# Block-causal attention with a gated FFN: q's and k's last 64 tokens in one tile and one transpose, and a planner that counts TensorE's weight loads

## The chip, the cores and the metric

The kernel runs on one core of a Trainium2 chip. The metric is the time of one execution on the device, in microseconds (us). The time before is 800.11 us, the median of three runs (797.95 to 801.85).

## What is computed

Eight batches of eight heads attend over 576 tokens with 64 dimensions per head. A token sees its own block of 64 and all earlier ones. The heads' results, side by side, are the 512-wide input of a feed-forward net: a matmul to 1024, a ReLU, a convolution over three neighbouring tokens whose sigmoid gates the ReLU's output, and a matmul back to 512.

```python
scores = scale * np.matmul(q, k.transpose(0, 1, 3, 2))
mask = block_i >= block_j                    # blocks of 64 tokens
attn = softmax(np.where(mask, scores, -1e9))
x = np.matmul(attn, v)                       # heads side by side: (8, 576, 512)
h = np.maximum(x @ w_in, 0.0)
conv_out = sum(conv_w[k] * hp[:, k:k + S, :] for k in range(3))
out = (h * sigmoid(conv_out)) @ w_out
```

## The kernel before

**Number format.** TensorE multiplies in fp32r. Where that is too coarse, a value is kept as a high part and a low part (`qh` and `ql`, `kh` and `kl`, `xh` and `xl`, `gh` and `gl`, and so on), and a product is summed from two or three matmuls.

**Visits.** Two heads together (a pair) are 128 partitions wide. The work on one pair is a visit. The first batch's four pairs are visited twice, for the tokens up to 256 (part A) and for the rest (part B), so that work can begin while the FFN's weights still arrive. The other 28 pairs have one visit each.

**A visit.** `load_nat` (L493) loads q and k of the pair with tokens on partitions, into the buffers `qn` and `kn`, of which there is one each. 576 tokens are four chunks of 128 and a fifth of 64, so the fifth chunk's tile fills only partitions 0 to 63. `chunks` (L488, the call is L491) turns each chunk by a transpose on TensorE: the tile is the stationary operand (the weights), an identity is the moving one. For the fifth chunk weights and identity are cut to 64 rows. `stage_t` (L804) does that in four PSUM banks, two for q (chunks 0 to 2, then 3 and 4) and two for k. ScalarE copies each bank out as a high part (L824), VectorE writes the low part (L827), and DMAs that SyncE issues (L837, L846, L857) put the halves in place. In part B `rest_t` (L896) does the same for chunks 2 to 4, in one bank for q and one for k. Then come scores in four steps of 128 queries (`stage_s`, L1022 and L1024, tile `s`, two banks) and one step for the last 64 queries of both heads (`last_s`, L977), with maximum (VectorE L1032), exponential (ScalarE L1035) and normalisation (GpSimd L951); transposes of the probabilities (`stage_x`, L1208, tile `w`, three banks); and the product with V (`stage_pv`, L1299, with one short product for the last chunk, L1295). That product has a first pass with 128 columns of weights (V's high and low part side by side) and a second pass, for the probabilities' low part, with 64 columns of weights.

**The FFN.** `ffn` (L1353) makes the net's matmuls (L1375 into 1024 features, L1434 back, tile `f`) for half a batch at a time. They are `paced`: spread over the attention of the next batch.

**The planner.** Every step of all these is an `Op` with an engine, a length that formulas such as `c_mm` and `c_tr` give, and what it depends on. `Plan.forward` (L163) plays the whole program through and takes on each engine the ready step that is due first; `Plan.late` turns the result into new due times, and `order` (L151) keeps the best of 25 rounds. What comes out is the order in which each engine's instructions are written; the chip then runs each engine's queue in that order. Where the plan has TensorE idle for over 0.4 us it puts in filling matmuls that compute nothing (L1565), which keep its clock up. Before the change a matmul's planned length is that of its moving operand alone:

```python
    def c_mm(n, m=P):
        return max(n * 0.000447 + 0.005, 0.086 * m / P)

    def c_tr(n):
        return max(n * 0.083 - 0.035, 0.06)
```

In `stage_pv` the second pass is one step in the plan, or two of up to two matmuls each: `halves` (L1282, L1286).

Of the kernel before, what the change touches and what calls it, by code (L numbers as in the profile page):

```python
# [10 lines left out]
F32R = mybir.dt.float32r  # L11
# [8 lines left out]
class Op:  # L20
    __slots__ = ("eng", "dur", "lat", "fn", "deps", "target", "seq", "outs", "left", "start", "end", "paced", "port", "xfer", "area", "rows64")
# [41 lines left out]
class Plan:  # L63
# [5 lines left out]
    SIGNAL = (0.055, 0.035, 0.035, 0.08, 0.1)  # L69
# [15 lines left out]
    def op(self, eng, dur, fn, target, deps=(), bufs=(), lat=0.0, paced=False, port=False, xfer=0.0, area=0.92,  # L85
           rows64=False):
        o = Op()
        o.xfer, o.area, o.rows64 = xfer, area, rows64
        o.port = port or eng == POOL
# [61 lines left out]
    def order(self, window, skip, fill, clock, rounds):  # L151
        best, least = None, 1e30
        for _ in range(rounds + 1):
            done = self.forward(window, skip, fill, clock)
# [8 lines left out]
    def forward(self, window, skip, fill, clock):  # L163
# [41 lines left out]
        rtime = [0.0] * len(self.ops)  # L205
        port = 0.0
# [4 lines left out]
        while left:  # L211
# [5 lines left out]
            for e in range(5):  # L217
# [26 lines left out]
            if e == PE and t - free[PE] > least and t > begin:  # L244
# [11 lines left out]
                if banks:  # L256
# [3 lines left out]
                    if k > 0:  # L260
# [3 lines left out]
                        x.area, x.rows64 = 0.91, False  # L264
                        use(x)
# [5 lines left out]
            if where == 0:  # L271
                heapq.heappop(ready[e][0 if o.port or o.paced else 1])
# [18 lines left out]
            for c in o.outs:  # L291
                c.left -= 1
                lat = self.DRAIN[e] + (self.SIGNAL[c.eng] if c.eng != e else 0.0) if (e != PE or c.eng != PE) else 0.0
                rtime[c.seq] = max(rtime[c.seq], o.end + o.lat + lat)
                if c.left == 0:
# [6 lines left out]
def kernel(  # L302
# [74 lines left out]
    ROUNDS = 24  # L377

# [48 lines left out]
    spans = [(f"p{i}", 128 * (i + 1), 2) for i in range(4)] + [("p4", S, 1), ("qn", 5 * P, 1), ("kn", 5 * P, 1)]  # L427
# [18 lines left out]
    def c_mm(n, m=P):  # L446
        return max(n * 0.000447 + 0.005, 0.086 * m / P)

    def c_tr(n):
        return max(n * 0.083 - 0.035, 0.06)  # L450
# [37 lines left out]
    def chunks(n, tb, cs):  # L488
        for z, c in enumerate(cs):
            m = P if c < 4 else 64  # L490
            nc.tensor.transpose(tb.ap[:, P * z:P * z + m].bitcast(F32R), n.raw[0:m, P * c:P * c + P], rident[0:m, 0:m])  # L491

    def load_nat(p, at, part=None):  # L493
        b, h0 = p // NP, 2 * (p % NP)
        c0 = 2 if part else 0
        res = []
        for src, tag in ((q, "qn"), (k, "kn")):
            n = twin(tag)

            def go(src=src, n=n):  # L500
                x = n.ap.rearrange("p (c j d) -> p c j d", c=5, j=2)
# [3 lines left out]
                nc.sync.dma_start(out=x[0:64, 4, :, :], in_=src[b, h0:h0 + 2, 4 * P:S, :].rearrange("j p d -> p j d"))  # L505

            res.append((n, pl.op(SP, 1.5, go, at, bufs=[n], xfer=c_dma(2 * (S - P * c0) * D * 4, 256))))
# [160 lines left out]
    def split(f, parts, src, hi, lo, scratch, deps, bufs, at, go):  # L668
# [52 lines left out]
        o2 = pl.op(PE, c_mm(512), less, at + 1, deps=[o1], bufs=[fb])  # L721
        if f in WPA:
            o2 = pl.op(PE, 4 * c_mm(512), all_, at + 1, deps=[o2], bufs=bufs + [fb])
        o2 = pl.op(PE, c_mm(512), rest, at + 1, deps=[o2] + [x[1] for x in o], bufs=bufs + [fb])
# [78 lines left out]

    def stage_t(nat, at):  # L804
# [5 lines left out]
        for which, (n, ld) in enumerate(nat):  # L810
            hi, lo = (qh, ql) if which == 0 else (kh, t["kl"])
            scale = SCALE if which == 0 else 1.0
            t0 = at + 2.0 * which
            es = []
            for j, cs in enumerate(((0, 1, 2), (3, 4))):
                tb = bank("tv")
                nn = (384, 192)[j]
                tok = slice(384 * j, 384 * j + nn)

                def tr(n=n, tb=tb, cs=cs):  # L820
                    chunks(n, tb, cs)

                def ev_hi(tb=tb, hi=hi, scale=scale, tok=tok, nn=nn):
                    nc.scalar.activation(out=hi.ap[:, tok], in_=tb.ap[:, 0:nn], func=AF.Copy, scale=scale)  # L824

                def ev_lo(tb=tb, hi=hi, lo=lo, scale=scale, tok=tok, nn=nn):
                    nc.vector.scalar_tensor_tensor(out=lo.ap[:, tok], in0=tb.ap[:, 0:nn], scalar=scale,  # L827
                                                   in1=hi.ap[:, tok], op0=ALU.mult, op1=ALU.subtract)

                o = pl.op(PE, c_tr(len(cs)), tr, t0 + 0.5 * j, deps=[ld], bufs=[n, tb], area=0.7)  # L830
                o = pl.op(ACT, c_act(nn) + 0.03, ev_hi, t0 + 0.5 * j + 0.3, deps=[o], bufs=[tb, hi])
                es.append(o)
                es.append(pl.op(DVE, c_dve(nn, two_in=True), ev_lo, t0 + 0.5 * j + 0.7, deps=[o], bufs=[tb, hi, lo]))
# [62 lines left out]
    def rest_t(nat, at):  # L896
# [4 lines left out]
        for which, (n, ld) in enumerate(nat):  # L901
            hi, lo = (t["qa"], t["qb"]) if which == 0 else (t["kh"], t["kl"])
            scale = SCALE if which == 0 else 1.0
            for j in range(1):
                tb = bank("tv")
                nn = S - Q1
                tok = slice(Q1, S)

                def tr(n=n, tb=tb):
                    chunks(n, tb, (2, 3, 4))  # L910

                def ev_hi(tb=tb, hi=hi, scale=scale, tok=tok, nn=nn):
                    nc.scalar.activation(out=hi.ap[:, tok], in_=tb.ap[:, 0:nn], func=AF.Copy, scale=scale)

                def ev_lo(tb=tb, hi=hi, lo=lo, scale=scale, tok=tok, nn=nn):
                    nc.vector.scalar_tensor_tensor(out=lo.ap[:, tok], in0=tb.ap[:, 0:nn], scalar=scale,
                                                   in1=hi.ap[:, tok], op0=ALU.mult, op1=ALU.subtract)

                t0 = at + 0.5 * (which + j)
                o = pl.op(PE, c_tr(3), tr, t0, deps=[ld], bufs=[n, tb], area=0.7)  # L920
                o = pl.op(ACT, c_act(nn) + 0.03, ev_hi, t0 + 0.3, deps=[o], bufs=[tb, hi])
                es.append(o)
                es.append(pl.op(DVE, c_dve(nn, two_in=True), ev_lo, t0 + 0.7, deps=[o], bufs=[tb, hi, lo]))
# [40 lines left out]
    def last_s(t, ready4, t0, pb, done, exps, part):  # L964
# [4 lines left out]
        for j in range(2):  # L969
# [12 lines left out]
            o = pl.op(PE, 3 * c_mm(HS), mm4, t0, deps=ready4, bufs=[sb, t["qz"], t["qdl"], t["kh"], t["kl"]])  # L982
# [17 lines left out]
    def stage_s(ops, hh, at, part, shared):  # L1000
# [9 lines left out]
        for z, i in enumerate(i for g in groups for i in g):  # L1010
# [27 lines left out]
            o = pl.op(PE, 2 * c_mm(nk) + (0.05 if i == 0 else 0) + (0.09 if pmask else 0), mm, t0, deps=ready[hh],  # L1038
# [14 lines left out]
    def stage_sb(ops, at):  # L1053
# [4 lines left out]
        for z, i in enumerate((2, 3)):  # L1058
# [15 lines left out]
            m = pl.op(PE, 3 * c_mm(nk) + 0.06, mm, t0, deps=ready, bufs=sb + [t[x] for x in ("qa", "qb", "kh", "kl")],  # L1074
# [527 lines left out]
```

## Time and profile before

| what | value |
|---|---|
| median of three runs | 800.11 us |
| the profiled execution | 800.5 us |
| its span, first to last instruction | 798.7 us |
| mean granted TensorE clock | 0.996 |
| busy: TensorE matmul (PE) | 784.3 us, 98% |
| busy: TensorE weight load (PEld) | 698.8 us, 87% |
| busy: VectorE, ScalarE, GpSimd | 642.2, 617.8, 427.4 us |
| matmuls, of them filling ones | 5307, 90 |

How to read it. A matmul is two instructions. One loads the weights (PEld in the profile), the other streams the moving operand (PE). Both engines' rows overlap, because loads go ahead of the matmul before. The end of a matmul is modelled, so "PE busy" hides short stops. What tells how fast TensorE really goes are the starts of the weight loads: in a full queue one load starts each time that one matmul makes way. A timeline row `217.76 0.42 PEld L491 LDWEIGHTS ... x2` says that a group of two loads of line 491 began at 217.76 us and that the last of them ended 0.42 us later. Shapes are rows\*columns of the weights, then the operand.

### The profile page before, as it was taken

Reading aid. Unit: us, or ns where it says so; the run is one execution under the profiler, and the core shown is the slowest. Engines: PE = TensorE matmul, PEld = TensorE weight load, DVE = VectorE, ACT = ScalarE, POOL = GpSimd, SP = SyncE. Lnnn points to the kernel's source line nnn. Section 1 sums busy time; section 2 is a strip of 40 time slices with the busy share of each in tenths; the row PEclk is TensorE's granted clock in tenths of the full one; section 3 lists DMA queues with packets and bytes.
Section 4 is the critical chain, followed back from the end, with each engine's and each line's share of the span. In section 5 each row is a group of like instructions: output and inputs, shape, how many; then the busy total and the mean of one; then the engine's idle time right before and its main releaser. Section 6 shows DMA issues by size and latency. Waiting matters only on the chain.

```text
span 798.7 us, 17165 instructions
## 1 busy us (share of the span) xinstructions
PE 784.3 (98%) x5307; PEld 698.8 (87%) x5307; DVE 642.2 (80%) x1889; ACT 617.8 (77%) x1769; POOL 427.4 (54%) x607
## 2 busy tenths in 40 slices
PE   7999999999999999999999999999999999999998
PEld 4678789888989889898989889898999989898996
DVE  6789988998988869797888869888888959887541
ACT  4779888877978769797887859787887858787652
POOL 3436545566664645555456644645565643646431
PEclk9899999999999999999999999999999999999999
DMA  9423465557555445445555454455554445540001
GB/s 247 130 56 101 119 148 122 139 124 171 124 125 137 103 115 129 112 114 121 137 132 118 98 130 111 119 124 136 128 125 106 111 111 123 126 107 15 14 27 39
DMA packets 164350, 91.34 MB, mean 114 GB/s; under 512 B 135564, under 2 KB 139684, under 8 KB 164260
## 3 DMA queue, kind: packets, MB, share of 16 engines
q1 hardware_dynamic: 163716, 90.12, 46.8%
q8 instruction: 43, 0.70, 0.4%
q14 instruction: 47, 0.39, 0.2%
q10 hardware_dynamic: 544, 0.13, 0.1%
HBM read 38.30 MB, written 9.44 MB: 60 GB/s over the span
## 4 chain that ended last, share of the span: by engine, by line
PE 91%; DVE 4%; ACT 2%; POOL 1%; DMA 1%; issue 1%; SPq 0%; ACTq 0%; POOLq 0%; DVEq 0%
PE f L1375 25%; PE f L1434 22%; PE w L1299 12%; PE w L1208 7%; PE s L1022 5%; PE s L1024 4%; PE w L491 4%; PE w L1434 4%; PE s L977 3%; PE s L1375 2%; PE s L1068 1%; DMA gh<-in_moe_w_in_dram 1%; PE s L1565 0%; PE w L1224 0%; POOL p0f L1164 0%
## 5 line engine op out<-in xcount | busy, mean ns | idle before, releaser
L1415 POOL TENSOR_TENSOR gl<-t,gh 128x288 fp32r<-128x288 f32 (+2 forms) x128 | 103.5, 812 | 148.6 <-ACT gh L1412 131.2
L1032 DVE TENSOR_REDUCE st<-s 128x1 f32<-128x128 f32 x224 | 107.1, 481 | 2.6
L1218 ACT ACTIVATE ptbh<-w 128x384 fp32r<-128x384 f32 (+2 forms) x192 | 94.5, 508 | 16.7 <-PE w L1208 15.5
L1434 PE MATMUL f<-woh,gh 128*128 128x512 f32 x248 | 103.8, 419 | 0.0
L1434 PE MATMUL f<-wol,gh 128*128 128x512 f32 x248 | 97.8, 394 | 0.0
L1434 PE MATMUL f<-woh,gl 128*128 128x512 f32 x248 | 97.8, 394 | 0.0
L1221 DVE TENSOR_TENSOR ptbl<-w,ptbh 128x512 fp32r<-128x512 f32 (+1 forms) x144 | 89.9, 628 | 9.1 <-ACT ptbh L1218 7.9
L1375 PE MATMUL f<-xh,wih 128*128 128x290 f32 (+2 forms) x480 | 95.5, 307 | 0.3 <-ACT p1f L1149 0.3
L1375 PE MATMUL f<-xh,wil 128*128 128x290 f32 (+2 forms) x480 | 95.3, 303 | 0.0
L1375 PE MATMUL f<-xl,wih 128*128 128x290 f32 (+2 forms) x480 | 92.4, 304 | 0.0
L951 POOL TENSOR_SCALAR p0f<-p0f,st 128x128 f32<-128x128 f32 x56 | 20.9, 373 | 121.4 <-DVE st L945 82.7
L1375 PEld LDWEIGHTS f<-xh,wil 128*128 128x128 f32 x480 | 73.7, 189 | 1.8 <-issue 0.2
L1396 DVE SCALAR_TENSOR_TENSOR t<-f,cw,t 128x287 f32<-128x287 f32 (+3 forms) x120 | 59.4, 496 | 19.5 <-ACT t L1392 17.9
L1375 PEld LDWEIGHTS f<-xh,wih 128*128 128x128 f32 x480 | 72.2, 189 | 2.3 <-ACT p1f L1149 0.8
L1375 PEld LDWEIGHTS f<-xl,wih 128*128 128x128 f32 x480 | 71.8, 189 | 0.9
L1024 PE MATMUL s<-kl,qz 128*128 128x128 f32 x224 | 72.1, 322 | 0.0
L1313 ACT ACTIVATE xt<-w 64x256 f32<-64x256 f32 x112 | 44.7, 402 | 29.4 <-PE w L1299 27.5
L1316 DVE TENSOR_TENSOR xt<-w,xt 64x256 f32<-64x256 f32 x112 | 51.4, 460 | 16.7 <-ACT xt L1313 13.4
L1392 ACT ACTIVATE t<-f,cw 128x288 f32<-128x288 f32 (+2 forms) x120 | 59.7, 499 | 2.7 <-ACT ptbh L1218 0.2
L1400 DVE SCALAR_TENSOR_TENSOR t<-f,cw,t 128x288 f32<-128x288 f32 (+3 forms) x120 | 60.4, 504 | 1.1
L1412 ACT ACTIVATE gh<-t 128x288 fp32r<-128x288 f32 (+2 forms) x128 | 56.3, 442 | 6.1 <-DVE t L1408 5.8
L1405 ACT ACTIVATE t<-t 128x288 f32<-128x288 f32 (+2 forms) x128 | 56.4, 442 | 5.9 <-DVE t L1400 5.3
(248 smaller groups left out, 2288.2 us busy)
## 6 DMA issues: line engine op xcount, KB each, us to landing
out_dram<-stage SPq DMA_DIRECT2D x36, 256.0 KB, 2.3
vn<-in_v_dram SPq DMA_DIRECT2D x64, 128.0 KB, 2.6
ka<-kh SPq DMA_DIRECT2D x56, 144.0 KB, 2.6
kb<-kh SPq DMA_DIRECT2D x56, 144.0 KB, 2.6
qnf<-in_q_dram SPq DMA_DIRECT2D x56, 128.0 KB, 2.5
knf<-in_k_dram SPq DMA_DIRECT2D x56, 128.0 KB, 2.7
qa<-qh SPq DMA_DIRECT2D x28, 144.0 KB, 2.4
qz<-qh SPq DMA_DIRECT2D x28, 144.0 KB, 2.6
```

The costliest lines, as they stand in the source:

```text
L1024: nc.tensor.matmul(sb.ap[:, 0:nk], qz.ap[:, z:z + 128], kl.ap[:, 0:nk], start=False, stop=True)
L1032: nc.vector.tensor_reduce(out=st.ap[:, i:i + 1], in_=sb.ap[:, 0:nk], op=ALU.max, axis=AX.X, negate=True)
L1218: nc.scalar.activation(out=hi(), in_=src(), func=AF.Copy)
L1221: nc.vector.tensor_tensor(out=lo(), in0=src(), in1=hi(), op=ALU.subtract)
L1299: nc.tensor.matmul(tb.ap[0:m, q0 - qa:qb - qa], vv.ap[:, chunk(c), hh, w[ps_]], pm.ap[:, 128 * c + q0:128 * c + qb] if qa == 0 else pm.ap[ ...
L1375: nc.tensor.matmul(fb.ap[:, 0:n2], wt[:, c, fs], xs[c][xi].ap[:, x0:x0 + n2], start=(n + c - c0 == 0), stop=(n + c - c0 == 3 * NCC - 1))
L1392: nc.scalar.activation(out=t.ap[:, 0:no], in_=fb.ap[:, own:own + no], func=AF.Copy, scale=cw[:, NFC + f:NFC + f + 1])
L1396: nc.vector.scalar_tensor_tensor(out=t.ap[:, i0:no], in0=fb.ap[:, own + i0 - 1:own + no - 1], scalar=cw[:, f:f + 1], in1=t.ap[:, i0:no], o ...
L1400: nc.vector.scalar_tensor_tensor(out=t.ap[:, 0:i1], in0=fb.ap[:, own + 1:own + 1 + i1], scalar=cw[:, 2 * NFC + f:2 * NFC + f + 1], in1=t.a ...
L1405: nc.scalar.activation(out=t.ap[:, 0:no], in_=t.ap[:, 0:no], func=AF.Tanh)
L1415: nc.gpsimd.tensor_tensor(out=gbuf[1].ap[:, f, carry:carry + no], in0=t.ap[:, 0:no], in1=gbuf[0].ap[:, f, carry:carry + no], op=ALU.subtract)
L1434: nc.tensor.matmul(fb.ap[:, 0:DM], gbuf[a].ap[:, f, cs], w[:, f, :], start=(f == 0 and n == 0), stop=(f == NFC - 1 and n == 2))
```

## The change

It has three parts.

1. **One tile for the two fifth chunks.** k's last 64 tokens are loaded into partitions 64 to 127 of q's fifth tile, and `kn` shrinks to four chunks. One transpose of 128 rows turns both; its output goes to two places of one bank, 64 columns each. `chunks` is gone; `naturals` does the transposes of both stages. `stage_t` now has three banks of three transposes (the middle one holds chunk 3 of q, the shared tile and chunk 3 of k, and is copied out in two pieces), `rest_t` a bank of three and one of two. k's load now writes into both buffers, so it also waits for the readers of `qn`.
2. **Planned lengths count weight loads.** Each matmul has a stream time and a load time (`mm_`, `tr_`); in the plan a matmul starts no earlier than its load's time after the one before it began, and a group's length is the sum over neighbours of the greater of stream and next load (`run`). Between ready steps `forward` now also looks at this: after a long stream, steps with a full-width load are brought forward by 1.0 us (`FAR`). `SIGNAL` of TensorE goes from 0.055 to 0.04. No other constant of the plan changes.
3. **V's second pass matmul by matmul.** In the visits after the first batch each matmul of the second pass is a step of its own.

```diff
-    SIGNAL = (0.055, 0.035, 0.035, 0.08, 0.1)
+    SIGNAL = (0.04, 0.035, 0.035, 0.08, 0.1)
...
+                if b and e == PE:
+                    near, far = pair if tail < 0.1 else (0.0, pair[1])
+                    b = min((x[2] for x in ready[e][1]),
+                            key=lambda o: (o.target - near if o.ldw < 0.06 else o.target - (0 if tail < 0.1 else far), o.seq))
...
             if e == PE:
+                o.start = t = max(t, max(begun, wtime[o.seq]) + o.ldw)
                 o.end = t + (o.dur + (switch if o.rows64 != rows else 0.0)) * speed(t)
+                begun, tail = o.end - o.tail * speed(t), o.tail
...
+    NEAR, FAR = 0.0, 1.0
...
-    spans = [(f"p{i}", 128 * (i + 1), 2) for i in range(4)] + [("p4", S, 1), ("qn", 5 * P, 1), ("kn", 5 * P, 1)]
+    spans = [(f"p{i}", 128 * (i + 1), 2) for i in range(4)] + [("p4", S, 1), ("qn", 5 * P, 1), ("kn", 4 * P, 1)]
...
+    def run(*mms):
+        total = sum(max(s, w) for (s, _), (_, w) in zip(mms, mms[1:])) + mms[-1][0]
+        return total, mms[0][1], mms[-1][0]
+
+    def mm_(n, m=P):
+        return 0.002 + n * 0.0004545, 0.001 + 0.000836 * m
+
+    def tr_(m=P, n=P):
+        return 0.002 + n * 0.0004545, 0.022 + 0.0005 * m
...
-    def chunks(n, tb, cs):
-        for z, c in enumerate(cs):
-            m = P if c < 4 else 64
-            nc.tensor.transpose(tb.ap[:, P * z:P * z + m].bitcast(F32R), n.raw[0:m, P * c:P * c + P], rident[0:m, 0:m])
...
-                nc.sync.dma_start(out=x[0:64, 4, :, :], in_=src[b, h0:h0 + 2, 4 * P:S, :].rearrange("j p d -> p j d"))
+                x = ns[0].ap[64 * z:64 * z + 64, 4 * P:5 * P].rearrange("p (j d) -> p j d", j=2)
+                nc.sync.dma_start(out=x, in_=src[b, h0:h0 + 2, 4 * P:S, :].rearrange("j p d -> p j d"))
...
+                for col, x, c in cs:
+                    o, m = tb.ap[:, col:col + P], rident
+                    if c == 4:
+                        o = tb.ap[:, col:col + 2 * x].rearrange("p (j n) -> p j n", j=2)[:, :, 0:64]
+                        x, m = nq, rident.rearrange("p (j n) -> p j n", j=2)
+                    nc.tensor.matmul(o.bitcast(F32R), x.raw[:, P * c:P * c + P], m, start=(col == 0), stop=True,
+                                     is_transpose=True, skip_group_check=True)
...
+        parts = ((((0, nq, 0), (P, nq, 1), (2 * P, nq, 2)), [lq], [nq], ((0, 0, 0, 384),)),
+                 (((0, nq, 3), (P, 192, 4), (192, nk, 3)), [lq, lk], [nq, nk], ((0, 0, 384, 192), (1, 192, 384, 192))),
+                 (((0, nk, 0), (P, nk, 1), (2 * P, nk, 2)), [lk], [nk], ((1, 0, 0, 384),)))
...
-                    halves = [h[::-1] for h in halves[::-1]]
+                    halves = [h[::-1] for h in halves[::-1]] if early else [[c] for c in cs[::-1]]
...
-                    cost = sum(c_mm(qb - max(128 * c, qa), m) for c in half) + (c_mm(64, m) if tailed else 0)
+                    cost = run(*([mm_(64, passes[k - 1][1])] if tailed else []), *[mm_(qb - max(128 * c, qa), m) for c in half])
```

The other changed lines of the diff put `run`, `mm_` and `tr_` in the place of `c_mm` and `c_tr`.

More of the change, by code (lines that the diff above doesn't have):

```diff
@@ L264, in forward @@
                         x.area, x.rows64 = 0.91, False
+                        begun, tail = x.end - each, each
                         use(x)
@@ L271, in forward @@
             if where == 0:
-                heapq.heappop(ready[e][0 if o.port or o.paced else 1])
+                h = ready[e][0 if o.port or o.paced else 1]
+                if h[0][2] is o:
+                    heapq.heappop(h)
+                else:
+                    h.remove(next(x for x in h if x[2] is o))
+                    heapq.heapify(h)
             else:
@@ L720, in split @@
             o1 = pl.op(ACT, c_act(512), fh, at + 1, deps=[x[0] for x in o], bufs=bufs)
-        o2 = pl.op(PE, c_mm(512), less, at + 1, deps=[o1], bufs=[fb])
+        o2 = pl.op(PE, run(mm_(512)), less, at + 1, deps=[o1], bufs=[fb])
         if f in WPA:
-            o2 = pl.op(PE, 4 * c_mm(512), all_, at + 1, deps=[o2], bufs=bufs + [fb])
-        o2 = pl.op(PE, c_mm(512), rest, at + 1, deps=[o2] + [x[1] for x in o], bufs=bufs + [fb])
+            o2 = pl.op(PE, 4 * mm_(512)[0], all_, at + 1, deps=[o2], bufs=bufs + [fb])
+        o2 = pl.op(PE, run(mm_(512)), rest, at + 1, deps=[o2] + [x[1] for x in o], bufs=bufs + [fb])
         if f in WPA:
@@ L809, in stage_t @@
         ready, ready4 = ([], []), []
-        for which, (n, ld) in enumerate(nat):
-            hi, lo = (qh, ql) if which == 0 else (kh, t["kl"])
-            scale = SCALE if which == 0 else 1.0
-            t0 = at + 2.0 * which
[L814 to L833, printed above, removed]
+        (nq, lq), (nk, lk) = nat
+        parts = ((((0, nq, 0), (P, nq, 1), (2 * P, nq, 2)), [lq], [nq], ((0, 0, 0, 384),)),
+                 (((0, nq, 3), (P, 192, 4), (192, nk, 3)), [lq, lk], [nq, nk], ((0, 0, 384, 192), (1, 192, 384, 192))),
+                 (((0, nk, 0), (P, nk, 1), (2 * P, nk, 2)), [lk], [nk], ((1, 0, 0, 384),)))
+        both = naturals(parts, nq, (qh, ql, kh, t["kl"]), (at, at + 0.5, at + 2.0))
+        for which in range(2):
+            t0 = at + 2.0 * which
+            es = both[which]
             if which == 0:
@@ L900, in rest_t @@
         es, ready4 = [], []
-        for which, (n, ld) in enumerate(nat):
-            hi, lo = (t["qa"], t["qb"]) if which == 0 else (t["kh"], t["kl"])
[L903 to L923, printed above, removed]
+        (nq, lq), (nk, lk) = nat
+        parts = ((((0, nq, 2), (P, nq, 3), (2 * P, 64, 4)), [lq, lk], [nq], ((0, 0, Q1, 320), (1, 320, 512, 64))),
+                 (((0, nk, 2), (P, nk, 3)), [lk], [nk], ((1, 0, Q1, 256),)))
+        both = naturals(parts, nq, (t["qa"], t["qb"], t["kh"], t["kl"]), (at, at + 0.5))
+        for which in range(2):
+            hi, lo = (t["qa"], t["qb"]) if which == 0 else (t["kh"], t["kl"])
+            t0 = at + 0.5 * which
+            es += both[which]
             if which == 0:
@@ L1570 @@
     ctx.enter_context(tc.manual_schedule(engines=None))
-    for o in pl.order(WINDOW, SKIP, (work, NBANK, 0.234, LEAST, SPARE), CLOCK, ROUNDS):
+    for o in pl.order(WINDOW, SKIP, (work, NBANK, 0.234, LEAST, SPARE), CLOCK, ROUNDS, (NEAR, FAR)):
         o.fn()
```

72 lines of the change are left out of this document (45 added, 27 removed).

## The prediction, made before the change was timed

> **What bounds the kernel now.** I read the page first, then busy time by stretches, then the groups by line and shape for TensorE's weight loads, and last the timeline of those loads. The page:
>
> ```profile
> span 798.7 us, 17165 instructions
> PE 784.3 (98%) x5307; PEld 698.8 (87%) x5307; DVE 642.2 (80%) x1889; ACT 617.8 (77%) x1769; POOL 427.4 (54%) x607
> ...
> PE 91%; DVE 4%; ACT 2%; POOL 1%; DMA 1%; issue 1%; SPq 0%; ACTq 0%; POOLq 0%; DVEq 0%
> ```
>
> TensorE bounds it: 91% of the chain that ended last is its work. The stretches (length, then busy us of PE, PEld, DVE, ACT, POOL, then the granted clock) tell where:
>
> ```profile
> 0.00:47.00 47.00, 40.42 (x208) 28.73 (x208) 33.48 (x98) 29.17 (x81) 20.82 (x37) 0.93 0.63 163
> 47.00:120.00 73.00, 70.01 (x498) 58.58 (x499) 66.19 (x184) 62.21 (x174) 38.74 (x62) 1.00 0.46 115
> ...
> 200.00:700.00 500.00, 499.88 (x3461) 454.72 (x3460) 417.50 (x1251) 401.32 (x1164) 280.60 (x390) 1.00 0.51 120
> ```
>
> From 200 to 700 us PE is never idle, at full clock, while VectorE is busy for 417.5 of 500 and ScalarE for 401. There each nanosecond that leaves TensorE's queue should leave the span. "Busy" still hides stops, since ends of matmuls are modelled; the starts of weight loads show them. Two healthy places, as start and length of each group of loads:
>
> ```profile
> 301.02 0.36 PEld L1208 LDWEIGHTS w<-rident,p2r 128*128 128x128 f32 x3
> 301.33 0.19 PEld L1022 LDWEIGHTS s<-ka,qa 128*128 128x128 f32 x1
> 301.44 0.19 PEld L1024 LDWEIGHTS s<-kl,qz 128*128 128x128 f32 x1
> 301.55 0.30 PEld L1375 LDWEIGHTS f<-xl,wih 128*128 128x128 f32 x2
> ...
> 302.30 0.45 PEld L1208 LDWEIGHTS w<-rident,p3r 128*128 128x128 f32 x4
> 302.69 0.30 PEld L1375 LDWEIGHTS f<-xh,wih 128*128 128x128 f32 x2
> ```
>
> Three transposes take 0.31 us to the next load (301.02 to 301.33), four 0.39 (302.30 to 302.69): 0.08 us for each further one, and so 0.14 to 0.15 for a run of one. Ordinary weights of 128 columns behind a short stream cost 0.11 (301.33, 301.44, 301.55). Now two places with a fifth chunk, a transpose of 64 rows (line 491):
>
> ```profile
> 195.05 0.14 PEld L491 LDWEIGHTS w<-rident,qnr 128*128 128x128 f32 x1
> 195.35 0.49 PEld L491 LDWEIGHTS w<-rident,qnr 64*128 64x128 f32 x4 [0.16 <-issue]
> 195.78 0.19 PEld L1434 LDWEIGHTS f<-woh,gh 128*128 128x128 f32 x1
> ...
> 217.76 0.42 PEld L491 LDWEIGHTS w<-rident,qnr 128*128 128x128 f32 x2
> 218.22 0.30 PEld L1375 LDWEIGHTS f<-xl,wih 128*128 128x128 f32 x2
> ```
>
> At 217.76 one whole and one 64-row transpose take 0.46 us where one whole takes 0.14: the 64-row one costs 0.32. At 195.05 one whole, one 64-row and three whole take 0.73 (to 195.78), against 0.39 for four whole: 0.34. The load path stands still in front of it (0.16 us, "issue": nothing is waited for) and the next load comes late too. That this holds for all 64 of them is in the groups by shape (busy, mean ns, idle before):
>
> ```profile
> L491 PEld LDWEIGHTS w<-rident,knr 128*128 128x128 f32 x120 | 14.5, 140 | 1.6 <-issue 0.2
> L491 PEld LDWEIGHTS w<-rident,qnr 128*128 128x128 f32 x120 | 14.1, 141 | 0.9
> L491 PEld LDWEIGHTS w<-rident,qnr 64*128 64x128 f32 x32 | 4.3, 136 | 4.6 <-issue 2.9
> L491 PEld LDWEIGHTS w<-rident,knr 64*128 64x128 f32 x32 | 4.3, 135 | 4.0 <-issue 0.5
> ```
>
> 8.6 us of idle stand before 64 loads of 64 rows (0.134 us each), 2.5 us before 240 loads of 128 rows (0.010 each).
>
> **The change part by part.** *The shared transpose.* It removes 64 transposes of 64 rows and adds 32 of 128 rows. In the order of TensorE at 194.5 to 195.8 us of the profile before, `qnr` and `knr` being q's and k's natural tiles:
>
> ```order
> L1295 MATMUL w<-ptbh,vv 128x64
> L1299 MATMUL w<-ptbl,vv 64x192
> L1299 MATMUL w<-ptbl,vv 64x320 x3
> L491 MATMUL w<-rident,qnr_95 128x128
> L491 MATMUL w<-rident,qnr_95 128x64
> L491 MATMUL w<-rident,qnr_95 128x128 x3
> L1434 MATMUL f<-woh,gh 128x512
> ```
>
> and the same visit in the changed kernel:
>
> ```order
> L832 MATMUL w<-rident,qnr_95 128x128
> L832 MATMUL w<-rident,qnr_95 128x2x64
> L832 MATMUL w<-rident,knr_97 128x128
> L1316 MATMUL w<-ptbh,vv 128x320 x3
> L1316 MATMUL w<-ptbh,vv 128x192
> L1312 MATMUL w<-ptbh,vv 128x64
> L1316 MATMUL w<-ptbl,vv 64x192
> L1316 MATMUL w<-ptbl,vv 64x320
> L832 MATMUL w<-rident,qnr_95 128x128 x3
> ```
>
> The 64-wide tail of q (and k's, further on) is gone, and the middle bank, with the 2x64 output, holds both. Removed: 64 x 0.32 = 20.5 us (19.2 to 21.8 by 0.30 and 0.34). Added: 32 x 0.08 = 2.6 us, since all rows are now 128. Net -17.9 us. At the least, if only the idle time in front goes and the 32 fewer loads, it is 8.6 + 32 x 0.08 = 11.2 us. 56 of the 64 belong to the 28 visits after the first batch, where TensorE bounds all.
>
> Here the Trainium skill bears on the row: "TensorEngine Tiling (Array Packing)", section Tiling Modes, says that a change of the tiling mode, not merely of the tile, drains TensorE. Row and rule agree that going to 64 rows and back stops the queue. The same page counts weights of 64 columns as another mode too; by that the next part would cost stops. The trace speaks against it:
>
> ```profile
> 324.43 0.38 PEld L1208 LDWEIGHTS w<-rident,p2r 128*128 128x128 f32 x3
> 324.75 0.19 PEld L1299 LDWEIGHTS w<-ptbl,vv 128*64 128x64 f32 x2
> 324.95 0.19 PEld L1434 LDWEIGHTS f<-woh,gh 128*128 128x128 f32 x1
> 325.09 0.19 PEld L1434 LDWEIGHTS f<-wol,gh 128*128 128x128 f32 x1
> ```
>
> *V's second pass.* Here two loads of 64 columns follow a transpose with no stop. They take 0.20 us together. The second interval streams 320 columns, as the next one does (324.95 to 325.09, 0.14); so the first took 0.06. Behind a transpose a narrow load costs 0.06 where a wide one costs 0.11. In the order such places rise from 13 to 40: 27 x 0.05 = -1.4 us. TensorE near 188.4 to 190.5 us, before (`p0r` to `p3r` probabilities, `vv` V):
>
> ```order
> L1295 MATMUL w<-ptbh,vv 128x64
> L1299 MATMUL w<-ptbl,vv 64x192
> L1299 MATMUL w<-ptbl,vv 64x320 x3
> L1208 MATMUL w<-rident,p0r_79 128x128
> L1208 MATMUL w<-rident,p1r_83 128x128 x2
> L1022 MATMUL s<-ka,qa 128x384
> L1024 MATMUL s<-kl,qz_127 128x384
> L1208 MATMUL w<-rident,p2r_87 128x128 x3
> L1434 MATMUL f<-woh,gh 128x512
> L1434 MATMUL f<-wol,gh 128x512
> L1434 MATMUL f<-woh,gl 128x512
> L1022 MATMUL s<-ka,qa 128x512
> ```
>
> and now:
>
> ```order
> L1312 MATMUL w<-ptbh,vv 128x64
> L1316 MATMUL w<-ptbl,vv 64x192
> L1316 MATMUL w<-ptbl,vv 64x320
> L1225 MATMUL w<-rident,p0r_79 128x128
> L1225 MATMUL w<-rident,p1r_83 128x128 x2
> L1316 MATMUL w<-ptbl,vv 64x320
> L1039 MATMUL s<-ka,qa 128x384
> L1041 MATMUL s<-kl,qz_127 128x384
> L1225 MATMUL w<-rident,p2r_87 128x128 x3
> L1316 MATMUL w<-ptbl,vv 64x320
> L1039 MATMUL s<-ka,qa 128x512
> ```
>
> The three narrow products have moved apart, each behind a run of transposes.
>
> *The new plan.* The same rows show its price: the three 512-wide FFN products no longer stand ahead of the 512-wide scores, which need the bank that the scores of 256 keys filled. They gave that bank's maximum and exponential this much time:
>
> ```profile
> 189.87 0.19 PEld L1434 LDWEIGHTS f<-woh,gh 128*128 128x128 f32 x1
> ...
> 190.44 0.19 PEld L1022 LDWEIGHTS s<-ka,qa 128*128 128x128 f32 x1
> ```
>
> 0.57 us. A score bank is free again after mask, maximum and exponential; the longest is 0.11 + 0.68 + 0.69 us, and today the score products wait little:
>
> ```profile
> L1022 PEld LDWEIGHTS s<-ka,qa 128*128 128x128 f32 x112 | 21.0, 188 | 3.7 <-issue 1.6 <-ACT p3f L1035 0.4 <-ACT p2f L1035 0.3
> L1022 PEld LDWEIGHTS s<-kb,qb 128*128 128x128 f32 x112 | 21.0, 187 | 4.0 <-ACT p4f L991 1.8 <-ACT p1f L1035 0.5
> L1029 DVE MEMSET s<- 64x64 f32 x224 | 24.9, 112 | 32.3 <-PE s L1024 25.7 <-ACT p1f L1035 1.7 <-PE w L1208 1.3
> L1032 DVE TENSOR_REDUCE st<-s 128x1 f32<-128x512 f32 x56 | 38.2, 681 | 0.3
> L1035 ACT ACTIVATE p3f<-s,st 128x512 f32<-128x512 f32 x56 | 38.5, 688 | 4.8 <-DVE st L1032 4.4
> ```
>
> 7.7 us of idle now stand before them. I take +3 us, some 40% more, between -2 and +8 (doubled). That is the least certain term. The filling matmuls fall from 90 to 72. A filler costs time only if real work behind it was ready:
>
> ```profile
> L1565 PE MATMUL s<-rident 128*128 128x512 f32 x83 | 28.6, 458 | 1.6 <-DVE rident L467 1.6
> ```
>
> 28.6 us for 83 makes at most 18 x 0.34 = 6.2 us, at the least 0. As the start waits for weights on other engines, I take -1.
>
> *At nothing:* ScalarE and VectorE copy out the same columns in as many pieces in 28 visits, and one piece more each in four; they have slack (first rows). k's load waits on SyncE's queue also for q's transposes, with q's and k's copies and stores queued behind it. SyncE already waits there:
>
> ```profile
> SPq L503 <- PE w L491: 111.4, 22, 9.1
> ```
>
> 111 us of such waits have held up nothing that TensorE shows, and the later reader, the middle bank, has a whole visit's time. If that cover were gone it would cost up to the load's landing, some us in a visit.
>
> The sum against the profiled execution, 800.5 us (span 798.7 and 1.8 around it; 0.4 above the median of 800.11): 800.5 - 17.9 - 1.4 - 1 + 3 = 783.2, or 783.
>
> **The rivals.** *The stop is not the rows' but the tile's.* Natural tiles come from a DMA and might stop TensorE at their second transpose whatever its shape. Then the shared one stops it as well: 32 stops of 0.24 (0.32 less 0.08) stay, 7.7 us, and the time is 791. Against it: whole ones inside 195.35 to 195.78 run on at the common pace. A cousin is the plain rule of the Trainium skill's "TensorE: Matmul & The Clock Gate", section LDWEIGHTS, that a load's time goes with its columns and not its rows. What that mechanism makes here, from rows: only 32 loads of 0.08 and 1.4 us go, and with the new waits it is 799. The idle of 8.6 us speaks against that.
>
> *Another engine takes over.* In 500 us VectorE is busy 417.5; with 483 of TensorE's time that is 86%. If its bursts then set the pace in half the visits, half the gain goes: 792.
>
> *Slower: score banks come too late.* With 28 visits of ten score banks (eight steps and two halves) there are 280 refills. A mean wait of 0.07 us more on each eats the 20 us; from 0.09 the change is slower by over 0.5%, and at 0.1 (28 us) the time is 800.5 - 20.3 + 28 = 808. The shorter distance in the order speaks for some of it, the idle of 7.7 us in all, over 280, against nearly four times that.
>
> **How the numbers follow.** Chances: forecast 0.75; stop stays in part, or other engines take half, 0.15 (791, 792); no stop saved, 0.04 (799); slower 0.04 (808); the rest, 0.02, better than all that. The forecast's own bounds: best -21.8 - 1.4 - 6.2 - 2 + 2.6 gives 772, worst -11.2 + 8 gives 797; both ends at once are unlikely, so 774 to 793, which takes in the second case. About 0.5% (4 us) is what a measurement of this kernel can tell from no change: faster below 796.1, 0.90; within, 0.06; slower, 0.04.
>
> **What would show it.** Right: no idle in front of natural loads of line 832 beyond 0.01 us each; whole runs at 0.08 to 0.09 each; the middle bank no longer than three transposes; narrow products at 0.06 behind transposes. The period of the batches between 200 and 700 us shrinks by about 2 us each. Wrong: loads of L832 with "issue" before them, or score loads (L1039) with over 15 us of idle.

## The result, and the profile after

The changed kernel takes 780.84 us (median of four runs, 779.7 to 781.83) against 800.65 us for the kernel before on the same chip: a ratio of 0.9757, 95% interval 0.9728 to 0.9786, so 17 to 22 us faster. The forecast was 783, between 774 and 793. The profiled execution took 781.83 us, with a span of 780.1 against 798.7. One execution each of full_rows and far_zero, further down, ran at a granted clock near 0.66 and took 1000 us or more; their times below are medians of the others, and full_rows has no start and middle there, since that execution was its profiled one.

First the page of the changed kernel, then its stretches, as before (length, busy us of PE, PEld, DVE, ACT, POOL, granted clock):

```profile
span 780.1 us, 17121 instructions
PE 762.3 (98%) x5257; PEld 684.7 (88%) x5257; DVE 645.2 (83%) x1893; ACT 612.1 (78%) x1773; POOL 428.8 (55%) x607
...
PE 84%; DVE 8%; ACT 4%; DMA 2%; issue 1%; POOL 1%; SPq 0%; ACTq 0%; DVEq 0%; POOLq 0%
```

```profile
0.00:47.00 47.00, 40.21 (x229) 28.58 (x230) 39.58 (x113) 30.88 (x88) 22.80 (x41) 1.00 0.65 171
47.00:120.00 73.00, 67.59 (x495) 56.48 (x495) 67.03 (x189) 63.93 (x184) 39.33 (x64) 1.00 0.47 119
...
200.00:700.00 500.00, 499.98 (x3532) 461.59 (x3532) 429.44 (x1281) 408.30 (x1196) 286.52 (x397) 1.00 0.52 123
```

TensorE still bounds the long middle: 499.98 of 500 us, with 3532 matmuls where 3461 stood before. VectorE rises from 417.5 to 429.4 us of the 500, 86%, without becoming the bound. In the first 47 us the clock is now full (1.00 where it was 0.93), which the forecast did not reckon with.

The loads of the natural tiles, grouped by shape (busy, mean ns, idle before), have lost their stop:

```profile
L832 PEld LDWEIGHTS w<-rident,qnr 128*128 128x128 f32 x152 | 17.8, 140 | 3.0 <-DVE st L1100 1.3
L832 PEld LDWEIGHTS w<-rident,knr 128*128 128x128 f32 x120 | 14.7, 141 | 1.4 <-DVE xt L1333 0.2
```

4.4 us before 272 loads, 0.016 each, and 1.3 of it is one single wait; before the change 8.6 us stood before the 64 loads of 64 rows alone. A middle bank with the shared tile, and V's narrow loads behind three transposes, in the timeline of weight loads (start, length of the group):

```profile
189.98 0.38 PEld L832 LDWEIGHTS w<-rident,qnr 128*128 128x128 f32 x3
190.30 0.19 PEld L1316 LDWEIGHTS w<-ptbl,vv 128*64 128x64 f32 x2
190.50 0.19 PEld L1451 LDWEIGHTS f<-woh,gh 128*128 128x128 f32 x1
...
213.17 0.28 PEld L832 LDWEIGHTS w<-rident,qnr 128*128 128x128 f32 x2
213.39 0.14 PEld L832 LDWEIGHTS w<-rident,knr 128*128 128x128 f32 x1
213.48 0.19 PEld L1039 LDWEIGHTS s<-kb,qb 128*128 128x128 f32 x1
```

From 213.17 to 213.48 three transposes, the shared one among them, take 0.31 us, as three whole ones did at 301.02 before. The two narrow loads at 190.30 take 0.20 us, as at 324.75 before.

Where the 18.6 us of span came from shows at two marks. One is the first load of the second batch's net, the other the first one into tile `s` in the last batch's net. Before:

```profile
197.68 0.30 PEld L1375 LDWEIGHTS f<-xh,wih 128*128 128x128 f32 x2
```

```profile
L1375 PEld LDWEIGHTS s<-xh,wih x32: 187/191/193, 742.8 to 776.8; 128*128 128x128 f32 x32
```

After:

```profile
193.34 0.30 PEld L1392 LDWEIGHTS f<-xh,wih 128*128 128x128 f32 x2
```

```profile
L1392 PEld LDWEIGHTS s<-xh,wih x32: 187/188/193, 723.9 to 758.2; 128*128 128x128 f32 x32
```

The start is 4.3 us shorter (197.7 to 193.3), the middle 14.5 (545.1 to 530.6), and the end the same within 0.3 us (55.9, 56.2). The middle is six batches long, at full clock before and after, so a batch in it takes some 2.4 us less; about 2 were forecast.

### The profile page after: what moved, and what is told of

The parts are those of the page before. It is cut to its first block, busy times and chain, and to the rows that moved or that the text cites. A ratio compares the mean times of both kernels' runs of the same rounds, so it can differ in the third digit from the quotient of the medians.

```text
span 780.1 us, 17121 instructions
## 1 busy us (share of the span) xinstructions
PE 762.3 (98%) x5257; PEld 684.7 (88%) x5257; DVE 645.2 (83%) x1893; ACT 612.1 (78%) x1773; POOL 428.8 (55%) x607
## 4 chain that ended last, share of the span: by engine, by line
PE 84%; DVE 8%; ACT 4%; DMA 2%; issue 1%; POOL 1%; SPq 0%; ACTq 0%; DVEq 0%; POOLq 0%
PE f L1392 23%; PE f L1451 22%; PE w L1316 11%; PE w L1225 7%; PE s L1039 5%; PE s L1041 4%; PE w L1451 4%; PE s L994 3%; PE w L832 2%; PE s L1392 2%; DMA ka<-kh 1%; DVE st L1100 1%; DMA gh<-in_moe_w_in_dram 1%; DVE t L1413 1%; DVE ptbl L1238 1%
## 5 line engine op out<-in xcount | busy, mean ns | idle before, releaser
L1235 ACT ACTIVATE ptbh<-w 128x384 fp32r<-128x384 f32 (+2 forms) x192 | 92.9, 512 | 11.3 <-PE w L1225 10.7
L1392 PE MATMUL f<-xh,wil 128*128 128x290 f32 (+2 forms) x480 | 91.9, 301 | 0.0
L1392 PE MATMUL f<-xh,wih 128*128 128x290 f32 (+2 forms) x480 | 91.0, 303 | 0.0
L1392 PE MATMUL f<-xl,wih 128*128 128x290 f32 (+2 forms) x480 | 89.1, 300 | 0.0
L968 POOL TENSOR_SCALAR p3f<-p3f,st 128x512 f32<-128x512 f32 x56 | 39.1, 698 | 36.7 <-DVE st L962 33.6
```

The costliest lines, as they stand in the source:

```text
L968: nc.gpsimd.tensor_scalar(out=pt.ap, in0=pt.ap, scalar1=st.ap[:, col:col + 1], scalar2=0.0, op0=ALU.mult, op1=ALU.add)
L1235: nc.scalar.activation(out=hi(), in_=src(), func=AF.Copy)
L1392: nc.tensor.matmul(fb.ap[:, 0:n2], wt[:, c, fs], xs[c][xi].ap[:, x0:x0 + n2], start=(n + c - c0 == 0), stop=(n + c - c0 == 3 * NCC - 1))
```

## The experiments

The theory on record: TensorE stops whenever the number of rows in use changes between 128 and 64, and that is most of the gain. The rivals: the tile or the DMA behind it causes the stop; or the new plan carries the gain. All times are medians, each beside runs of the kernel before on the same chip. Start and middle are those of the two marks above, in the profiled execution.

| run | us | ratio to before, 95% interval | start, us | middle, us |
|---|---|---|---|---|
| before | 800.65 | 1 | 197.7 | 545.1 |
| the change | 780.84 | 0.9757 (0.9728 to 0.9786) | 193.3 | 530.6 |
| full_rows | 786.68 | 0.9838 (0.9815 to 0.9861) | | |
| full_rows_again | 787.60 | 0.9856 (0.9839 to 0.9873) | 194.7 | 536.2 |
| two_halves | 788.60 | 0.9857 (0.9840 to 0.9874) | 194.8 | 536.9 |
| tile_only | 780.39 | 0.9752 (0.9737 to 0.9767) | 190.2 | 532.5 |
| tile_split | 797.28 | 0.9967 (0.9956 to 0.9979) | 196.7 | 543.1 |
| v_grouped | 783.14 | 0.9798 (0.9782 to 0.9815) | 193.5 | 531.5 |
| far_zero | 784.37 | 0.9813 (0.9794 to 0.9832) | 192.3 | 532.5 |
| tile_nofill | 784.69 | 0.9815 (0.9791 to 0.9839) | 195.1 | 532.5 |
| after_again | 779.87 | 0.9756 (0.9736 to 0.9775) | 191.0 | 530.7 |
| more_fill | 778.97 | 0.9742 (0.9724 to 0.9761) | 190.4 | 530.7 |
| far_two | 780.78 | 0.9769 (0.9747 to 0.9791) | 192.2 | 530.0 |
| hybrid | 784.00 | 0.9805 (0.9786 to 0.9825) | 194.6 | 532.4 |

The middle repeats well (530.6 and 530.7 in the two profiles of the changed kernel, 530.7 in more_fill, which has its order); the start does not (193.3, 191.0 and 190.4).

**full_rows and full_rows_again: the same order, whole tiles.**

```diff
-            m = P if c < 4 else 64
-            nc.tensor.transpose(tb.ap[:, P * z:P * z + m].bitcast(F32R), n.raw[0:m, P * c:P * c + P], rident[0:m, 0:m])
+            nc.tensor.transpose(tb.ap[:, P * z:P * z + P].bitcast(F32R), n.raw[:, P * c:P * c + P], rident)
...
+    for tag in ("qn", "kn"):
+        nc.gpsimd.memset(twins[tag][0][0][64:P, 4 * P:5 * P], 0.0)
```

> The kernel before, in its own order, with the 64 fifth chunks transposed as tiles of 128 rows (rows 64 to 127 are zeros, set once at the start; the extra output columns are not read). Same number of transposes, same order on every engine. Theory: the stop belongs to the change between 128 and 64 rows, 0.23 us for each of 64, so -15 us: 785.5 (783 to 788), and no idle before those loads. Rival, the natural tile itself stops TensorE, or a load's price goes by its columns alone: no change, 800 (798 to 802), idle before those loads as before.

> The same as full_rows (787.7 against 800.4), for a trace at full clock. Theory: the 64 loads lose their idle of 0.13 us in front and the next load comes 0.085 us after, not 0.175; span 14 to 15 us below the profile of before if the half-speed stretch of TensorE at 20 to 27 us of that profile belongs to this order and recurs, some 3 us more if it was chance and does not.

Measured: 13.7 us less, and 11.8 in the second run. The loads of full_rows_again by shape, and one place in its timeline with a chunk 3 and a fifth chunk of k behind p1's transposes:

```profile
L492 PEld LDWEIGHTS w<-rident,knr 128*128 128x128 f32 x152 | 18.3, 140 | 1.7 <-PE f L701 0.2 <-issue 0.2
L492 PEld LDWEIGHTS w<-rident,qnr 128*128 128x128 f32 x152 | 17.7, 140 | 1.9
```

```profile
195.62 0.23 PEld L1209 LDWEIGHTS w<-rident,p1r 128*128 128x128 f32 x2
195.79 0.22 PEld L492 LDWEIGHTS w<-rident,knr 128*128 128x128 f32 x2
195.96 0.30 PEld L1376 LDWEIGHTS f<-xh,wih 128*128 128x128 f32 x2
```

Both natural transposes take 0.17 us (195.79 to 195.96). Idle before all 304 natural loads is 3.6 us, where it was 11.1 (2.5 and 8.6). Tiles, DMAs and order are those of before. What changed is the row count and, with it, the width of the identity that is streamed, 64 columns to 128; that the narrow stream is not the cause shows in the next experiment. So the rows cause the stop, and the tile and its DMA do not. The size falls short of 15 us by 1 to 3, and the span by 11.9 us where 14 to 15 were expected. Idle before the score loads rises only from 7.7 to 8.2 us in this order, which explains little of that:

```profile
L1023 PEld LDWEIGHTS s<-ka,qa 128*128 128x128 f32 x112 | 21.1, 188 | 4.4 <-ACT t L1406 1.4 <-issue 0.9 <-ACT p3f L1036 0.4
L1023 PEld LDWEIGHTS s<-kb,qb 128*128 128x128 f32 x112 | 21.0, 187 | 3.8 <-ACT p4f L992 1.8 <-ACT p1f L1036 0.5
```

The clock explains more. The stretch of low clock in the start came again and was longer:

```profile
0.00:20.00 20.00, 15.23 (x61) 11.13 (x62) 11.56 (x40) 9.29 (x25) 8.49 (x18) 0.94 0.99 249
20.00:47.00 27.00, 25.66 (x148) 18.61 (x147) 22.23 (x58) 19.60 (x56) 12.43 (x22) 0.86 0.34 99
```

The granted clock, the number behind the five busy times, is 0.94 and 0.86 here; in the profile of before it was 1.00 and 0.87. By these shares some 1.5 us more are lost, an estimate, and that is half or more of what the span falls short by. The middle is free of it: 45 of the 64 short transposes lie there, and making them whole shortens it by 8.9 us (545.1 to 536.2, the marks below), 0.20 us each.

```profile
194.73 0.19 PEld L1376 LDWEIGHTS f<-xh,wih 128*128 128x128 f32 x1
```

```profile
L1376 PEld LDWEIGHTS s<-xh,wih x32: 187/191/192, 730.9 to 764.9; 128*128 128x128 f32 x32
```

**two_halves: is it each such transpose, or each change?**

```diff
...
                     if c == 4:
-                        o = tb.ap[:, col:col + 2 * x].rearrange("p (j n) -> p j n", j=2)[:, :, 0:64]
-                        x, m = nq, rident.rearrange("p (j n) -> p j n", j=2)
+                        for j, y in enumerate((nq, nk)):
+                            nc.tensor.matmul(tb.ap[:, col + x * j:col + x * j + 64].bitcast(F32R), y.raw[0:64, P * c:P * c + P],
+                                             rident[0:64, 0:64], start=False, stop=True, is_transpose=True, skip_group_check=True)
+                        continue
...
```

> The changed kernel, in its own plan, with k's last 64 tokens back in k's own tile and two 64-row transposes side by side in the middle bank where the one of 128 rows stood. Theory, a stop for each change of the row count and none between two of 64 rows: one way in and out for each of 32, 32 x (0.23 + 0.09) = 10 us more than 780.8: 791 (789 to 793). Rival, a stop for each transpose of 64 rows: 32 x (2 x 0.24 + 0.09) = 18 us more: 799. Second rival, no stop at all, only one more load: 783.

Measured: 788.6, 7.8 us above the changed kernel, 0.4 below the theory's range; both rivals, 799 and 783, are off by more than 5 us. A pair of 64-row transposes from two tiles costs one stop, not two: the middle is 6.3 us longer for 22 pairs, 0.29 each, which is 0.20 and one load more. The timeline of weight loads tells more than the time:

```profile
487.79 0.14 PEld L833 LDWEIGHTS w<-rident,qnr 128*128 128x128 f32 x1
488.07 0.14 PEld L830 LDWEIGHTS w<-rident,qnr 64*128 64x128 f32 x1
488.16 0.14 PEld L830 LDWEIGHTS w<-rident,knr 64*128 64x128 f32 x1
488.33 0.14 PEld L833 LDWEIGHTS w<-rident,knr 128*128 128x128 f32 x1
488.42 0.19 PEld L1040 LDWEIGHTS s<-kb,qb 128*128 128x128 f32 x1
```

Going in costs 0.28 us where 0.14 is usual behind a 290-wide stream. From one 64-row load to the next it is 0.09, the common pace, though the stream between them is only 64 columns wide. Going out costs 0.17 instead of 0.09. So it is the change that costs, twice, some 0.23 us together. The groups say the same for all 32:

```profile
L830 PEld LDWEIGHTS w<-rident,knr 64*128 64x128 f32 x32 | 4.4, 137 | 0.3 <-DMA knf<-in_k_dram 0.3
L830 PEld LDWEIGHTS w<-rident,qnr 64*128 64x128 f32 x32 | 4.3, 136 | 4.3 <-issue 1.7
```

4.3 us of idle before the first of each two, 0.3 before the second. The Trainium skill, "TensorEngine Tiling (Array Packing)", section Tiling Modes, says that a change of mode drains TensorE while a change of tile within one does not. These rows agree for 64 and 128 rows; for weights of 64 and 128 columns, which the page lists as modes too, the rows at 190.30 show no stop. Whether a load of 64 columns is run as such a mode at all, no row here shows.

**tile_only and tile_split: the tile without the plan, the plan without the tile.** In tile_only, `load_nat`, `naturals`, `stage_t` and `rest_t` are the new ones and the rest is the kernel before; in tile_split it is the other way round.

```diff
# tile_only, against the changed kernel
-            o = pl.op(PE, run(*[tr_()] * len(cs)), tr, t0, deps=lds, bufs=bufs + [tb], area=0.7)
+            o = pl.op(PE, c_tr(len(cs)), tr, t0, deps=lds, bufs=bufs + [tb], area=0.7)
...
# tile_split, against the changed kernel
-                 (((0, nq, 3), (P, 192, 4), (192, nk, 3)), [lq, lk], [nq, nk], ((0, 0, 384, 192), (1, 192, 384, 192))),
-                 (((0, nk, 0), (P, nk, 1), (2 * P, nk, 2)), [lk], [nk], ((1, 0, 0, 384),)))
+                 (((0, nq, 3), (P, nq, 4)), [lq], [nq], ((0, 0, 384, 192),)),
+                 (((0, nk, 0), (P, nk, 1), (2 * P, nk, 2)), [lk], [nk], ((1, 0, 0, 384),)),
+                 (((0, nk, 3), (P, nk, 4)), [lk], [nk], ((1, 0, 384, 192),)))
...
```

> The kernel before with the shared tile and transpose alone; planned lengths and V's second pass as before. Theory: the tile carries 17.9 us: 783 (780 to 786), nearly all of it after 200 us. Rival, the gain of the change is the new plan's: 795 to 800.

> The changed kernel with the two fifth tiles apart again, each with its 64-row transpose, in four banks; planned lengths and V's second pass stay new. Theory: the 64 stops come back, +17.9 on 780.8: 799 (795 to 802), and the first 200 us stay as short as in the changed kernel. Rival, the plan carries the gain: 783 to 786.

Measured: the tile alone gives 20.0 us, as much as the whole change; undoing it alone gives back 16.4 of the 19.5 or so, and leaves 3.1 us to the plan. The rival falls. The marks of tile_only, and of tile_split:

```profile
190.15 0.19 PEld L1371 LDWEIGHTS f<-xh,wih 128*128 128x128 f32 x1
```

```profile
L1371 PEld LDWEIGHTS s<-xh,wih x32: 187/191/193, 722.6 to 756.7; 128*128 128x128 f32 x32
```

```profile
196.71 0.30 PEld L1389 LDWEIGHTS f<-xh,wih 128*128 128x128 f32 x2
```

```profile
L1389 PEld LDWEIGHTS s<-xh,wih x32: 187/188/193, 739.8 to 774.1; 128*128 128x128 f32 x32
```

The middle of tile_only is 532.5 us long, 12.6 less than before, and its start 7.5 less. That the start would gain so much was not expected ("nearly all of it after 200 us" fails), nor that the start of tile_split would be 3.4 us longer than the changed kernel's. In the middle the two parts simply add up. The tile takes off 12.6 us in the old plan and 12.5 in the new one (543.1 to 530.6); the plan takes off 2.0 without the tile (545.1 to 543.1) and 1.9 with it. In the start they do not: tile_only's is the shortest of the four. In tile_split the stops are back (3.8 and 4.1 us of idle before its 64-row loads):

```profile
L828 PEld LDWEIGHTS w<-rident,qnr 64*128 64x128 f32 x32 | 4.4, 136 | 3.8 <-issue 1.2
L828 PEld LDWEIGHTS w<-rident,knr 64*128 64x128 f32 x32 | 4.3, 135 | 4.1 <-issue 0.9
```

**v_grouped and far_zero: the second pass and the preference.**

```diff
# v_grouped
-                    halves = [h[::-1] for h in halves[::-1]] if early else [[c] for c in cs[::-1]]
+                    halves = [h[::-1] for h in halves[::-1]]
# far_zero
-    NEAR, FAR = 0.0, 1.0
+    NEAR, FAR = 0.0, 0.0
```

> The changed kernel with V's second pass in steps of two matmuls, as before the change; tile and planned lengths stay. Narrow loads right behind a transpose fall from 41 to 33. Theory: 8 x 0.05 = 0.4 us and little else, 781 (780 to 782.5). Rival, the single steps let the plan avoid waits: 783 to 786.

> The changed kernel with FAR at 0: no preference for full-width loads after a long stream. Narrow loads behind transposes fall from 41 to 10. Theory: 31 x 0.05 = 1.6 us more, 782.5 (781 to 784). Rival, the preference costs as much in waits as it gains in loads: 780 to 781.

Measured: 783.1 and 784.4, against 780.8 and 779.9 in the two runs of the changed kernel. By the medians each is worth 2 to 5 us, more than 8 or 31 places of 0.05 us make; the theory's range is missed by both, and v_grouped falls into its rival's. The marks show what the medians hide. In the middle v_grouped is 0.9 us longer than the changed kernel and far_zero 1.9, near the theory's 0.4 and 1.6. The rival's waits are not there: idle before the score loads is 4.4 us in v_grouped and 2.8 in far_zero, where the changed kernel has 8.1. What is left lies in the start, and differs from one execution to the next: the spans of the profiled ones, 781.1 and 781.0, are 1 us above one profile of the changed kernel (780.1) and over 3 above the other (777.8).

**tile_nofill and more_fill: what a filling matmul costs.** In tile_nofill the fillers are left out of tile_only; in more_fill they are put in from shorter gaps on.

```diff
# tile_nofill
-            for _ in range(k):
-                nc.tensor.matmul(b.ap.rearrange("p (c n) -> p c n", n=P), x,
-                                 x.unsqueeze(1).broadcast_to([P, 4, P]), start=True, stop=True)
+            pass
# more_fill
-    LEAST, SPARE = 0.4, 0.09
+    LEAST, SPARE = 0.25, 0.05
```

> The shared tile alone (tile_only, 780.4) with all 99 filling matmuls left out and every other instruction where it was. Theory, the fillers stand in time in which TensorE waits anyway: the idle takes their place, 780 to 782. Rival, the prediction's term: a filler delays what is ready behind it, at most 99 x 0.34 us: 770 to 777. Second rival, without them TensorE's clock is granted by half in the first 47 us: 790 or more.

> The changed kernel with every real instruction where it was and 86 filling matmuls instead of 72 (put in from 0.25 us of planned idle on, not 0.4). Theory from tile_nofill, fillers stand in idle time and hold the clock, which is full here already: same as the changed kernel within 1 us. Rival, each filler delays what is ready behind it: 14 x 0.2 to 0.34, 3 to 5 us slower.

Measured: without fillers 784.7, 4.3 us slower than tile_only and between the ranges that were named; with 14 more 779.0, no slower than after_again's 779.9 (the intervals overlap). The 14 delay no work. The middle of tile_nofill is as long as tile_only's, so all that the fillers do, they do in the start. It shows in the stretches of tile_nofill and then of tile_only:

```profile
20.00:47.00 27.00, 20.41 (x113) 14.97 (x113) 23.17 (x63) 18.59 (x57) 11.06 (x20) 0.87 0.32 93
47.00:120.00 73.00, 65.71 (x468) 55.50 (x467) 65.76 (x178) 60.71 (x174) 37.18 (x62) 0.93 0.44 112
```

```profile
20.00:47.00 27.00, 24.35 (x156) 17.00 (x155) 23.84 (x67) 19.07 (x59) 11.57 (x21) 1.00 0.31 91
47.00:120.00 73.00, 69.53 (x518) 59.26 (x518) 68.34 (x187) 63.15 (x182) 40.78 (x68) 1.00 0.46 117
```

Without fillers the granted clock is 0.87 and 0.93 in the two stretches, with them 1.00.

**after_again, far_two and hybrid: a better version?**

```diff
# far_two
-    NEAR, FAR = 0.0, 1.0
+    NEAR, FAR = 0.0, 2.0
# hybrid: plain[0] is set for the first eight visits
+        if plain[0]:
+            return sum(s for s, _ in mms), 0.0, mms[-1][0]
         total = sum(max(s, w) for (s, _), (_, w) in zip(mms, mms[1:])) + mms[-1][0]
```

> The changed kernel itself, for a comparison on the same chip: 780.8 (779.5 to 782).

> The changed kernel with FAR at 2.0 instead of 1.0: narrow loads right behind transposes rise from 41 to 64. Theory: 23 x 0.05 = 1.2 us less in the steady part, start unknown within 2 us: 778 to 781. Rival, later probabilities and scores cost waits: 782 to 785.

> The changed kernel with lengths that leave weight loads out for the steps of the first eight visits, as the old planner had them there, and the new lengths from the ninth visit on; 99 fillers. Theory: the start of the tile alone (190 us to the second batch's net, 3 us less than now) with the steady part of the change (528 us, 2.5 us less than with the tile alone): 777 to 779. Rival, start and steady part are not separable: 780 to 783.

Measured: 779.9, 780.8 and 784.0. 23 more narrow loads behind transposes make the middle 0.6 us shorter (1.2 were expected) and bring nothing that the median could tell. A plan that counts loads only from the ninth visit on is slower than either case named for it: its start (194.6) and its middle (532.4) both miss what they were to have, and its clock between 20 and 47 us is 0.87. The best median is more_fill's 778.97, which its interval does not set apart from the change or from tile_only.

## Why the prediction was right

**The stop** (64 x 0.32 us gone): right in kind. Rows change, TensorE stops going in and going out; full_rows and two_halves show it. Alone it was worth 12 to 14 us where 15 were reckoned, and 0.20 us each in the middle where 0.23 stood (0.32 less one load).

**The shared tile** (-17.9): right where it can be measured cleanly. The middle holds 45 of the 64 places, so 12.6 of the 17.9 us; measured were 12.6 and 12.5. Not all of it is the stop. Between full_rows_again and tile_only the middle shortens by 3.7 us, and 22 or 23 fewer loads of 0.08 are only half of that; idle before the score loads also falls there, from 6.2 to 3.3 us. The other 4.6 us between the two lie in the start, where tile_only's clock stayed at 1.00 and that of full_rows_again dropped to 0.86.

**V's second pass** (-1.4): the price of a narrow load behind a transpose was right (0.20 us for two, again), and the middle bears the term out: the plan with the second pass takes 1.9 to 2.0 us off it. The median does not move (780.4; 780.8 and 779.9), because the start of the changed kernel is longer than tile_only's. The planner before was not quite blind to loads: its `c_mm` puts 0.086 us under a matmul whose weights have 128 columns.

**New waits** (+3): their place was wrong. Over the whole run the score loads of the changed kernel wait hardly longer than before, 8.1 us against 7.7:

```profile
L1039 PEld LDWEIGHTS s<-ka,qa 128*128 128x128 f32 x112 | 21.1, 188 | 5.8 <-ACT p3f L1052 1.8 <-DMA ka<-kh 1.4 <-ACT xt L1330 0.7
L1039 PEld LDWEIGHTS s<-kb,qb 128*128 128x128 f32 x112 | 21.0, 187 | 2.3 <-ACT p4f L1008 1.4 <-ACT p1f L1052 0.4
```

But from the first mark on they wait less, 2.6 us where it was 5.1, in spite of the shorter distance in the order; ahead of it they wait more, 5.6 us where it was 2.6 (3.8 in after_again). So the steady visits, from which the term was argued, do not have it, and the start has some of it. With that falls the rival "slower". For "another engine takes over" nothing speaks either: VectorE is busy for 86%, as reckoned, beside 499.98 us of TensorE in 500. In the whole run weight loads wait for VectorE for 7.4 us, 4.7 before.

**Fillers** (-1): the thought behind it was wrong. They cost nothing that more_fill could show, and leaving all of them out of tile_only costs 4.3 us.

**Not in the sum: the clock.** Between 20 and 47 us the kernel before had TensorE busy for 26.14 of 27 us at a granted clock of 0.87; the changed kernel has 1.00 there:

```profile
20.00:47.00 27.00, 26.14 (x150) 18.80 (x150) 20.02 (x56) 19.93 (x57) 12.93 (x25) 0.87 0.36 101
```

```profile
20.00:47.00 27.00, 23.46 (x164) 16.69 (x164) 25.84 (x72) 20.60 (x63) 13.18 (x24) 1.00 0.39 111
```

That is more than a chance of one execution. In the 28 runs of the kernel before that stand beside the experiments the mean clock is 0.991 to 0.998; those at 0.993 took 800.3 to 801.5 us, those at 0.998 took 797.7 to 798.0. The eight of the changed kernel have 0.997 to 1.000. A straight line through the 28 gives 0.55 us for each 0.001, so 2 to 3 us of the 20 go with the clock, an estimate. Why the new order keeps it is not shown.

So the hit is in part luck. In the middle, tile and second pass gave what was reckoned and the +3 was not needed. The start gave 4.3 us (6.7 in after_again), for which the forecast had 5.3 from the 19 other places of the tile and 1 from the fillers, although it also got the clock, which the sum did not have.

**Covered costs:** right as far as shown. SyncE's loads of q and k waited 111.4 us for TensorE's natural transposes; they now wait 38.4 us for those and 47.6 for score products, and TensorE's score loads wait for a DMA for 1.4 us in all.

Still open: why the start of the same kernel differs between executions (193.34 us to the second batch's net in one profile of the change, 190.96 in the other), and so which part of the start's 4.3 us belongs to the change; why tile_only's start is the shortest; and what v_grouped and far_zero lose outside the middle.

```profile
190.96 0.30 PEld L1392 LDWEIGHTS f<-xh,wih 128*128 128x128 f32 x2
```

## What to carry to other kernels

On a TensorE that looks busy for 100%, read the starts of the weight loads by shape: a small odd shape with idle time in front of it ("issue") is a stop that the busy row hides. Two half-height tiles that are handled alike are worth one full-height tile, less for the work than for the two changes of row count saved. Where one part of a change removes such a stop and another re-plans the whole order, run each alone and compare a steady stretch at full clock, not only the whole time: here 12.6 us of the middle's 14.5 were the first part's and 2 the second's, while by the medians the first seemed to be the whole gain.

## What the runs showed of the hardware that was not expected

- A change between weights of 128 and of 64 rows costs about 0.14 us going in and 0.08 to 0.09 going out in the rows of two_halves, and 0.20 us there and back on average (8.9 us for 45 in full_rows_again); two 64-row loads in a row cost nothing extra (0.09 us from one to the next), nor do weights of 64 columns among those of 128 (0.20 us for two, streams included).
- Without the 99 filling matmuls of tile_only, 97 of them in the first 120 us, the granted clock falls from 1.00 to 0.87 (20 to 47 us) and 0.93 (47 to 120 us), and the run takes 4.3 us more. Their number alone does not hold the clock: with 90 in the order of the kernel before it was 0.87 and 0.86 between 20 and 47 us in two profiles, with 99 in hybrid 0.87, and with 72 in the changed kernel 1.00.
